# Splits of token differences set free, and the first weight sums issued behind block 1's routing

## The chip, the cores and the metric

The kernel runs on one core of a Trainium2 chip. The metric is device microseconds of one launch. Five engines work beside each other, each through a queue of its own that it takes in order: TensorE (matrix products into PSUM), VectorE and ScalarE (elementwise work, the only ones of the four that read PSUM), POOL (elementwise work in SBUF), and SyncE, which issues most DMAs.

## The reference

Three layers are computed, one after the other.

```python
# 1: attention, 4 batches, 8 heads, 576 positions, 64 wide; banded or dilated mask
x = softmax(mask(q @ k.T / 8)) @ v            # -> 2304 tokens x 512
# 2: gated layer, 512 -> 1536 -> 512
x = (sigmoid(x @ w_gate) * (x @ w_val)) @ w_out
# 3: soft routing to 8 experts with 4 slots each
logits = x @ phi                              # 2304 x 32
d = softmax(logits, over tokens); c = softmax(logits, over slots)
slot_in = d.T @ x
slot_out = relu(slot_in[e] @ w1[e]) @ w2[e]   # for each expert e
out = c @ slot_out
```

The products of layer 2 are made from two-part numbers: every operand is split into a high half (rounded to the matrix engine's single-pass float32 form, `F32R`) and a low half (the difference), and a product is the sum of high by high, high by low and low by high.

## The kernel before, in words

Tokens come in five blocks n: blocks 0 to 3 are the first 512 tokens of the four batches, block 4 gathers the last 64 of each. The 1536 features of layer 2 come in twelve groups f of 128. Attention is made for pairs of units (block, pair of heads); block 0's is first, and the others run beside the gated layer of blocks 0 and 1 (`l1`, L515).

Blocks 2 and 3 are then done as a pair (`pair_l1`, L661). Their attention results stay unsplit, `xf[2]` and `xf[3]`, and the four products of a 2 by 2 block product (weights: gate and value, each in two halves of the 512 inputs; tokens: two blocks, each in the same two halves) are made from seven products of sums, so that a feature group takes 42 matrix instructions. The token sides of these seven are b11, b21 (`pair_x2`, the halves of block 2), b22 (`pair_x3`, a half of block 3) and the differences t1 to t4. `pair_sums` (L564) makes the differences on POOL, `pair_t` (L586) splits each into halves, in two column pieces: ScalarE casts the high half, VectorE subtracts for the low one (`split`, L552). The weight sides of a group are a11, a12, a22 and sums s1 to s4: class `PairW` (L599), with `sums1` to `sums3` on VectorE, the high halves on ScalarE, the low ones on VectorE and POOL (`low1`, `low2`).

After block n's gated layer comes its routing, `Post(n)`: eighteen steps. Logits and their exponentials; shares (the softmax over slots); twelve turns, each transposing one quarter of the features' results of 128 tokens on TensorE, with a copy out of PSUM, for block 1 always on ScalarE (L826); weights; and three gathers with the accumulation into `acc` (L864). `Post(0)` runs inside block 1's loop. `Post(1)` runs between block 1 and the pair, and the list `prep` is dealt out between its steps by `Spread`: of `len(prep)` items so many after each step that all are out three steps before the end.

Order. A planner fixes each engine's queue when the program is built: of the instructions that it takes to be ready, the earliest in the program goes first, so that work traced late can run early in a gap. `keep_in_program_order` ties an instruction behind the one traced just before it on the same engine, and behind that one alone. `kp` (L549) does so while `fixed[0]` is set, and `pinned` sets it around a call. Tiles are handed out by tag, and a tile's first writer waits until the last readers of the buffer's former tile are done: the two `qk` buffers held the last attention scores, the two `v` buffers the last values, and the two `xa` buffers hold `xf[2]` and `xf[3]`, after which b22 takes the first and the sums' tile `s` the second.

Of the kernel before, what the change touches and what calls it, by code (L numbers as in the profile page):

```python
# [60 lines left out]
def tile_kernel(  # L61
# [25 lines left out]
    def b8(tag, shape, dt, name):  # L87
        return big.tile(shape, dt, tag=tag, name=name, bufs=BUFS[tag])
# [463 lines left out]
    def split(eng, hi, lo, src_):  # L552
        kp(nc.scalar.copy(hi, src_))
        kp(eng.tensor_tensor(lo, src_, hi.bitcast(F32), ALU.subtract))
# [31 lines left out]
    def pair_t(z, c):  # L586
        name, at = (("t1", (0, 0)), ("t2", (2, 0)), ("t3", (0, 1)), ("t4", (2, 1)))[z]
        if c == 0:
            t = b8(("qk", "v")[z % 2], [P, 2, 2, 512], F32R, "t_hl")
            pair[name] = t[:, 0], t[:, 1]  # L590
        hi, lo = pair[name]
        split(nc.vector, hi[:, c], lo[:, c], pair["t", at[0]][:, at[1], c])
# [427 lines left out]
        prev_w[0].high2()  # L1020
        prev_w[0].low2()

    early_prep = [(pair_sums, z) for z in range(4)] + [(pair_t, z, c) for z in range(4) for c in range(2)]
    prep = [(pair_x2, z) for z in range(4)]
    prep += [(first_w,), (pair_x3, 0), (pair_x3, 1), (first_sums,), (first_splits,)]

    def pinned(fn, *args):
        fixed[0] = True
        fn(*args)
        fixed[0] = False  # L1030

    for x in early_prep:
        pinned(*x)
    prep = [(pinned, *x) for x in prep]
    after = after[mix0.done :] + Post(1).all()
    mix = Spread(prep, [(len(after) - 3, len(prep))])
    for fn, *args in after:
        fn(*args)
        mix()
    prev = None  # L1040
    w4 = []

# [57 lines left out]
    for f in range(NF):  # L1100
        c = f % 4
# [255 lines left out]
```

## Time and profile before

| | before |
|---|---|
| median of 3 runs | 498.23 us (497.89 to 499.33) |
| profiled execution | 498.77 us, span 496.8 us, mean granted clock 0.982 |
| TensorE products busy | 470.1 us, 95% of the span |
| VectorE, ScalarE, POOL busy | 301.4, 248.6, 158.3 us |
| chain that ended last | TensorE 76%, VectorE 3%, ScalarE 3% |
| moved by DMA | 112.13 MB, mean 226 GB/s |

The span is the time from the first to the last instruction of one profiled execution; its own time is 2 us longer, and runs differ by some tenths of a per cent. A busy TensorE isn't one at full speed: its products are pipelined, and the granted clock (1.00 is 2.4 GHz, 0.50 is 1.2 GHz) stands beside it in the windows. The place that the change touches is a small part of the span, so it is read from the windows and the timelines of that place, not from the shares of the whole.

### The profile page before, as it was taken

Reading aid. Unit: us, or ns where it says so; the run is one execution under the profiler, and the core shown is the slowest. Engines: PE = TensorE matmul, PEld = TensorE weight load, DVE = VectorE, ACT = ScalarE, POOL = GpSimd, SP = SyncE. Lnnn points to the kernel's source line nnn. Section 1 sums busy time; section 2 is a strip of 40 time slices with the busy share of each in tenths; the row PEclk is TensorE's granted clock in tenths of the full one; section 3 lists DMA queues with packets and bytes.
Section 4 is the critical chain, followed back from the end, with each engine's and each line's share of the span. In section 5 each row is a group of like instructions: output and inputs, shape, how many; then the busy total and the mean of one; then the engine's idle time right before and its main releaser. Section 6 shows DMA issues by size and latency. Waiting matters only on the chain.

```text
span 496.8 us, 12732 instructions
## 1 busy us (share of the span) xinstructions
PE 470.1 (95%) x5476; PEld 357.7 (72%) x5476; DVE 301.4 (61%) x561; ACT 248.6 (50%) x428; POOL 158.3 (32%) x132
## 2 busy tenths in 40 slices
PE   6789999999899999999889999999999999999993
PEld 3468877878677877877458888888887889643552
DVE  3969698967767353555956566556557665521522
ACT  2466566747666453546855545545435544300232
POOL 0243555635383321182143243342312134010100
PEclk9989999999999999999989999999999999989998
DMA  8979898979986501750020220220699795679997
GB/s 327 405 258 335 290 369 305 322 270 364 408 289 211 172 3 49 253 195 3 0 84 2 84 86 1 86 84 0 239 383 424 288 341 191 251 257 367 421 392 219
DMA packets 23784, 112.13 MB, mean 226 GB/s; under 512 B 2352, under 2 KB 7216, under 8 KB 14640
## 3 DMA queue, kind: packets, MB, share of 16 engines
q1 hardware_dynamic: 23408, 111.06, 60.1%
q8 instruction: 43, 0.70, 0.6%
q10 hardware_dynamic: 320, 0.26, 0.2%
q14 instruction: 13, 0.11, 0.1%
HBM read 97.16 MB, written 14.16 MB: 224 GB/s over the span
## 4 chain that ended last, share of the span: by engine, by line
PE 76%; DVE 3%; ACT 3%; issue 2%; DMA 1%; POOL 1%; SPq 0%; ACTq 0%; DVEq 0%; POOLq 0%
PE l1ps L527 27%; PE pa L651 13%; PE pe L651 6%; PE tp L821 4%; PE h_ps L1123 3%; PE pd L651 3%; PE xp L208 3%; PE so_ps L1182 2%; PE sp L852 2%; PE lt_ps L785 2%; PE s_ps L145 2%; PE wt_ps L468 1%; PE tr L188 1%; PE op L1221 1%; PE si_ps L1102 1%
## 5 line engine op out<-in xcount | busy, mean ns | idle before, releaser
L527 PE MATMUL l1ps<-x_hi,whl 128*128 128x512 f32 x384 | 129.5, 404 | 3.1 <-ACT x_hi L229 2.3
L527 PEld LDWEIGHTS l1ps<-x_hi,whl 128*128 128x128 f32 x384 | 72.2, 189 | 20.4 <-ACT x_hi L229 3.0
L527 PE MATMUL l1ps<-x_lo,whl 128*128 128x512 f32 x192 | 76.1, 397 | 0.0
L442 POOL TENSOR_TENSOR fw<-fw 128x512 int32<-128x512 int32 x36 | 51.4, 1437 | 71.5 <-DVE fw L441 35.1
L527 PEld LDWEIGHTS l1ps<-x_lo,whl 128*128 128x128 f32 x192 | 36.4, 190 | 7.2 <-issue 0.4
L539 DVE TENSOR_TENSOR g<-l1ps,g 128x512 f32<-128x512 f32 (+1 forms) x36 | 21.6, 600 | 32.7 <-PE l1ps L527 32.2
L527 PE MATMUL l1ps<-x,whl 128*128 128x256 f32 x288 | 37.2, 286 | 0.0
L527 PEld LDWEIGHTS l1ps<-x,whl 128*128 128x128 f32 x288 | 35.4, 191 | 2.1 <-issue 1.9
L537 ACT ACTIVATE g<-l1ps 128x512 f32<-128x512 f32 (+1 forms) x36 | 18.9, 526 | 30.2 <-PE l1ps L527 30.1
L494 POOL TENSOR_TENSOR whl<-w,whl 128x512 fp32r<-128x512 f32 x12 | 15.9, 1326 | 52.1 <-ACT whl L493 40.6
L821 PE MATMUL tp<-cst,g 128*128 128x128 f32 x216 | 28.6, 275 | 0.0
L494 POOL TENSOR_TENSOR whl<-wst,whl 128x512 fp32r<-128x512 f32 x12 | 16.1, 1340 | 38.6 <-ACT whl L493 33.9
L439 ACT ACTIVATE fw<-st 128x512 f32<-128x512 f32 x36 | 22.7, 675 | 10.9 <-DMA st<-wd 10.9
L821 PEld LDWEIGHTS tp<-cst,g 128*128 128x128 f32 x216 | 24.1, 140 | 3.6 <-ACT g L537 1.7
L494 DVE TENSOR_TENSOR whl<-fw,whl 128x512 fp32r<-128x512 f32 x24 | 22.0, 922 | 5.8 <-ACT whl L493 5.3
L720 DVE TENSOR_TENSOR tm<-pe,tm 128x512 f32<-128x512 f32 x12 | 8.3, 692 | 27.7 <-PE pe L651 27.7
L826 ACT COPY gt<-tp 128x512 f32<-128x512 f32 x33 | 18.5, 587 | 10.9 <-PE tp L821 9.3
L441 DVE TENSOR_SCALAR fw<-st 128x512 int32<-128x512 uint32 x36 | 22.6, 654 | 1.9 <-DMA st<-wd 1.9
L208 PEld LDWEIGHTS xp<-pt_ring,v 64*64 64x64 f32 x1216 | 19.2, 135 | 6.1 <-issue 4.0
L493 ACT CAST whl<-fw 128x512 fp32r<-128x512 f32 x24 | 14.7, 619 | 17.3 <-POOL fw L442 13.2
L440 DVE TENSOR_SCALAR fw<-fw 128x512 uint32<-128x512 uint32 x36 | 20.7, 584 | 2.7 <-ACT fw L439 2.2
L208 PE MATMUL xp<-pt_ring,v 64*64 64x32 f32 (+1 forms) x1216 | 20.7, 219 | 1.6 <-issue 0.9
(464 smaller groups left out, 961.2 us busy)
## 6 DMA issues: line engine op xcount, KB each, us to landing
ew<-w SPq DMA_DIRECT2D x32, 1024.0 KB, 7.9
st<-wd SPq DMA_DIRECT2D x18, 1024.0 KB, 9.0
wst<-wg SPq DMA_DIRECT2D x12, 1024.0 KB, 6.9
v<-qkv SPq DMA_DIRECT2D x20, 512.0 KB, 6.7
wg<-fw SPq DMA_DIRECT2D x12, 512.0 KB, 7.7
w<-wg SPq DMA_DIRECT2D x6, 1024.0 KB, 7.4
qk<-qkv SPq DMA_DIRECT2D x10, 576.0 KB, 6.4
qk<-qkv SPq DMA_DIRECT2D x8, 528.0 KB, 5.5
```

The lines of the kernel that those rows point to most:

```text
L208: nc.tensor.matmul(o, lhsT=v[k, t, i, r, :], rhs=p_[k, 2 * r + t, i, 0:nq], start=True, stop=True)
L439: nc.scalar.activation(top, st[:, c, 1].bitcast(F32), AF.Prelu, scale=2.0**-112, alpha=2.0**32)
L440: nc.vector.tensor_scalar(top.bitcast(U32), top.bitcast(U32), 3, None, ALU.logical_shift_left)
L441: nc.vector.tensor_scalar(low.bitcast(I32), st[:, c, 0], 2.0**-29, None, ALU.mult)
L442: nc.gpsimd.tensor_tensor(low.bitcast(I32), top.bitcast(I32), low.bitcast(I32), ALU.add)
L494: (nc.gpsimd if pool[h] else nc.vector).tensor_tensor(whl[:, 1, h], src[:, h], whl[:, 0, h].bitcast(F32), ALU.subtract)
L527: nc.tensor.matmul(pt[:, 0:nt], lhsT=whl[:, w_, a, dc, :], rhs=x_[n][:, dc, :], start=first, stop=(dc == HP_ORDER[-1] and w_ == 1),)
L537: nc.scalar.activation(g, pt[:, 0:nt], AF.Sigmoid)
L539: nc.vector.tensor_tensor(g, pt[:, 0:nt], g, ALU.mult)
L651: nc.tensor.matmul(pt, lhsT=w[:, w_, P * c : P * c + P], rhs=x_[:, c], start=first and c == 0 and w_ == 0 and x_ is hi, stop=c == 1 and w_ ...
L821: nc.tensor.transpose(tp[:, c], g_sb[self.n, 4 * q + c][:, P * j : P * j + P], ident)
L826: nc.scalar.copy(to, tp)
```

## The change

The four difference steps of `pair_sums` stay pinned. The eight calls of `pair_t` (sixteen instructions: eight on ScalarE, eight on VectorE) are traced at the same place in the program, but no longer pinned. `first_sums` and `first_splits`, which make the sums of group 0's weights and their halves, leave the list that is dealt out between the steps of `Post(1)` and are called, pinned, after the last of its steps. The list so has seven items instead of nine.

```diff
-    early_prep = [(pair_sums, z) for z in range(4)] + [(pair_t, z, c) for z in range(4) for c in range(2)]
     prep = [(pair_x2, z) for z in range(4)]
-    prep += [(first_w,), (pair_x3, 0), (pair_x3, 1), (first_sums,), (first_splits,)]
+    prep += [(first_w,), (pair_x3, 0), (pair_x3, 1)]
 
     def pinned(fn, *args):
         fixed[0] = True
         fn(*args)
         fixed[0] = False
 
-    for x in early_prep:
-        pinned(*x)
+    for z in range(4):
+        pinned(pair_sums, z)
+    for z in range(4):
+        for c in range(2):
+            pair_t(z, c)
     prep = [(pinned, *x) for x in prep]
     after = after[mix0.done :] + Post(1).all()
     mix = Spread(prep, [(len(after) - 3, len(prep))])
     for fn, *args in after:
         fn(*args)
         mix()
+    pinned(first_sums)
+    pinned(first_splits)
     prev = None
     w4 = []
```

## Rows read from the trace of the kernel before

**Rows 1.** Windows by stage: busy us of each engine, granted clock, DMA share, GB/s.

```profile
204.00:229.00 25.00, 25.00 (x376) 20.30 (x375) 12.27 (x23) 12.08 (x21) 15.02 (x12) 1.00 0.54 198
229.00:258.00 29.00, 24.85 (x222) 15.72 (x221) 22.17 (x48) 23.59 (x46) 6.74 (x7) 0.94 0.05 15
258.00:350.00 92.00, 92.00 (x407) 76.17 (x407) 57.83 (x99) 47.60 (x88) 32.18 (x30) 1.00 0.14 53
350.00:480.00 130.00, 128.77 (x1253) 91.08 (x1251) 65.56 (x133) 45.45 (x86) 22.52 (x19) 0.99 0.84 328
```

The columns are the window, its length, then PE, PEld, DVE, ACT and POOL (TensorE's products, its weight loads, VectorE, ScalarE, POOL).

**Rows 2.** Windows of 2 us in the passage to the pair stage.

```profile
238.00:240.00 2.00, 1.09 (x11) 0.85 (x9) 1.07 (x7) 1.97 (x5) 0.00 (x0) 1.00 0.00 0
...
248.00:250.00 2.00, 0.04 (x1) 0.04 (x1) 2.00 (x5) 0.81 (x4) 0.02 (x1) 1.00 0.00 0
250.00:252.00 2.00, 2.00 (x5) 1.42 (x6) 2.00 (x6) 0.53 (x2) 0.73 (x1) 0.51 0.00 0
252.00:254.00 2.00, 2.00 (x7) 0.93 (x5) 0.95 (x3) 1.64 (x3) 1.38 (x1) 0.63 0.00 0
```

**Rows 3.** Chain of waits from 225 to 275 us: start us, us, what.

```profile
231.66 2.78 PE lt_ps L785 x96
...
238.17 1.28 ACT L805
...
243.24 2.23 DVE b_lo L554 x3
...
252.62 2.02 POOL w__3366 L613
```

**Rows 4.** Timeline of POOL: start us, us, line, operation, count, idle before.

```profile
216.66 5.03 POOL L577 TENSOR_TENSOR tsum<-xf 128x512 f32<-128x512 f32 x4
221.66 5.02 POOL L577 TENSOR_TENSOR tsum<-xf,tsum 128x512 f32<-128x512 f32 x4
...
243.31 1.01 POOL L897 COPY pm<-c 128x512 f32<-128x512 f32 x1 [16.62 <-DVE c L891]
```

**Rows 5.** Timeline of TensorE from 223 to 259 us.

```profile
223.04 0.60 PE L188 MATMUL tr<-cst,qk 128*128 128x128 f32 x4
...
227.80 0.98 PE L208 MATMUL xp<-pt_ring,v 64*64 64x16 f32 x56
228.71 1.09 PE L821 MATMUL tp<-cst,g 128*128 128x128 f32 x8
...
231.61 2.83 PE L785 MATMUL lt_ps<-g,wp 128*32 128x128 f32 x96
...
244.82 1.07 PE L852 MATMUL sp<-gt,dt 128*32 128x512 f32 x8
...
258.06 0.39 PE L651 MATMUL pa<-b_hi,w__3466 128*128 128x512 f32 x1
```

**Rows 6.** Timeline of ScalarE from 228 to 253 us.

```profile
229.37 4.26 ACT L553 CAST t_hl<-tsum 128x512 fp32r<-128x512 f32 x8
...
239.57 0.29 ACT L809 ACTIVATE d<-d 128x128 f32<-128x128 f32 x1
...
241.00 3.10 ACT L826 COPY gt<-tp 128x512 f32<-128x512 f32 x6
245.55 1.14 ACT L553 CAST b<-xf 128x512 fp32r<-128x512 f32 x2 [1.45 <-DVE b_lo L554]
...
251.72 0.83 ACT L641 CAST w__3366<-s 128x768 fp32r<-128x768 f32 x1 [1.48 <-DVE s L613]
```

**Rows 7.** Timeline of VectorE from 232 to 250 us.

```profile
232.33 4.89 DVE L554 TENSOR_TENSOR t_hl<-tsum,t_hl 128x512 fp32r<-128x512 f32 x8
237.15 0.28 DVE L793 COPY lt<-lt_ps 128x128 f32<-128x128 f32 x1
...
245.39 1.39 DVE L864 SCALAR_TENSOR_TENSOR acc<-acc,nm,sp 128x512 f32<-128x512 f32 x2
...
249.05 0.75 DVE L613 TENSOR_TENSOR s<-wst 128x256 f32<-128x256 f32 x2
```

**Rows 8.** Line L554, the low halves of b22: ns min/median/max, first and last start.

```profile
L554 DVE TENSOR_TENSOR b<-xf,b x2: 679/952/1224, 246.7 to 247.3; 128x512 fp32r<-128x512 f32 x2
```

## The prediction

> **What bounds the kernel now.** I read the windows by stage first [rows 1]. From 258 to 350 us, the twelve features of the pair stage, TensorE is busy 92.00 of 92.00 us at full clock, and DMA moves little. From 350 on DMA works at a share of 0.84, with loads that start when the pair stage gives its buffers back, so whatever moves 258 moves the end by as much. From 204 to 229 TensorE is also full, while ScalarE is busy 12.08 of 25 us and VectorE 12.27. Only 229 to 258, the passage from block 1 into the pair stage, has room: TensorE 24.85 of 29, and there ScalarE (23.59) and VectorE (22.17) are the loaded ones. The fine windows show the holes [rows 2]: 0.91 us at 238 to 240, then TensorE nearly silent from 248 to 250, and after that its granted clock at 0.51 for two microseconds (half the slices at 1.2 GHz) and 0.63 in the next two.
>
> The chain of waits says who makes them [rows 3]. It goes from the logits product over the exponentials' table load to the three low halves of x2 (243.24), then to POOL's low half of the first weight sums (252.62). The gaps are filled from the engines' own queues [rows 4 to 7]. ScalarE casts the eight high halves of the differences from 229.37 for 4.26 us, ahead of all else [rows 6]. VectorE makes their eight low halves at 232.33 for 4.89 us, and only behind them, at 237.15, copies the logits that TensorE had finished at 234.44 [rows 5, 7]. The high halves of b22 wait 1.45 us for the last x2 low half, because b22 takes the buffer of xf[2] [rows 6]. The weight sums start at 249.05 [rows 7], because their tile takes the buffer of xf[3], which the low halves of b22 read last. From 249.05 it takes until 258.06 for the first product of feature 1 [rows 5].
>
> **The change, part by part.** *Splits free to move.* The halves need POOL's differences, done from 217.9 to 226.7 us (four in 5.03 and four in 5.02 us) [rows 4], and a buffer. t1 and t3 take the two qk buffers, read last by transposes of which the second group ends at 223.6 [rows 5]; t4 takes the v buffer that the last attention sums read until 228.78 [rows 5]; t2 waits for POOL alone, until 222.9 and 224.2. Unpinned, the planner may put them into the idle queue time of 217 to 229; that it lets work traced late run early is seen in POOL's copy at 243.31, which the code issues in the last stage [rows 4]. So six of eight high halves (0.53 us each) and six of eight low halves (0.61) go in front of 229, into ScalarE's 12.9 and VectorE's 12.7 idle microseconds of that stage [rows 1]. I cost them there at nothing; what it costs if that cover fails is the last rival.
>
> VectorE below costs 0.61 us per half, but a two-input operation beside POOL stretches: the low halves of b22 ran 679 and 1224 ns, the slow one beside POOL [rows 8]. The Trainium skill, "GPSIMD Engine Reference", section 1 (Specifications), says that POOL shares its SBUF interfaces with VectorE and that VectorE operations with two SBUF inputs contend with it; the trace agrees. It speaks against the change, since the low halves now run beside POOL's differences: by that rule and the row's 0.54 us six of them cost 3.3 us more, still inside the idle 12.7, and the sum stays.
>
> *What that gives VectorE.* With two low halves left (1.2 us, before 232.4), the logits' copy runs when the product ends, 234.5 instead of 237.15: 2.65 us earlier for the maximum, the exponentials and the shares.
>
> *What it gives ScalarE.* This is where the gain is lost again. From 229.4 it has two high halves (to 230.5), then two turned copies and one x2 high half that may go behind the first of them (to 232.4). After that it has nothing: TensorE is in the logits product until 234.4 and hands over the next turned group some 0.4 later, at 234.85 (two groups take 1.09 [rows 5]). From there ScalarE has ten turned copies (six take 3.10 us [rows 6]), three x2 high halves, one weight cast and two b22 high halves, 16 at 0.525 = 8.4 us, the table load of 1.28 [rows 3] and three small exponentials of 0.2, some 0.5: 10.2 us, to 245.0. Before, the last turned copy ended at 244.10 and the b22 high halves at 246.69 [rows 6]. So 3.2 us removed end as 1.7.
>
> *The x2 and b22 halves* now come at wider steps (7 pieces over 15 steps instead of 9), so the first weight cast stands behind the sixth turned group. It is in the 10.2 us; TensorE's first products wait for it but have until the weight sums. The last x2 low half waits for the shares, 2.65 us earlier, and ends before ScalarE reaches b22 at some 242, so that wait of 1.45 goes. Three turned copies stand behind the second b22 cast, which so ends at 243.4, and its low half near 244.2.
>
> *The first sums behind all steps of block 1.* sums1 is now tied to the last accumulate of block 1's routing. Before it was not: that ended at 246.78 [rows 7], 2.3 us ahead of the sums. Now it is what comes last: turned copy 245.0, four products 1.07 [rows 5], accumulate 0.70 (two in 1.39 [rows 7]): sums at 246.9 instead of 249.05, so **2.15 us** gained. Were the tie absent, they could start at 244.2; it costs 2.7 of what the first part offers. Behind the tied sums wait ScalarE's two casts and POOL's three low halves, whom TensorE waits for; in POOL's queue they pass nothing but the copy of 243.31, since the differences stay tied where they are.
>
> *Next feature's pieces.* The first low half and the first sums of feature 1 are tied behind VectorE's previous instruction, which was the accumulate and is now sums3 of feature 0. Before, feature 1's sums ran between those of feature 0: 249.05 to the cast at 251.72 is 2.67 us [rows 6, 7]. Four sums in a row at 0.42, with a hand-over, are 1.85 by estimate: **0.8 us** gained. The bounds are 0 (all of it latency) and 1.1 (four at 0.38, the pitch of the pair in rows 7). I take 0.8, near the upper end, because two foreign sums stood in between. No DMA is issued by a moved step, and SP's queue stays as it is.
>
> The sum is 2.15 + 0.8 = 3.0 us (rounded). The profiled execution took 498.77 us (span 496.8); 3.0 less is 495.8. It lies 0.54 above the median of the runs, 498.23, so I forecast **495.2 us**, with feature 1 starting at 255.1.
>
> A second rule concerns the table load. Here the load takes 1.28 us from 238.17, and the exponential at 239.57 is the second one behind it [rows 3, 6], so nothing more stands between. The Trainium skill, "ScalarE: Activation LUTs", "What ACT_TABLE_LOAD costs", adds a drain of about 1.38 us, 2.66 in all; by it ScalarE's list would end at 246.4 and the gain would be 1.6. This trace shows no such drain.
>
> **Rivals.**
> *More of it (gain 5.4).* ScalarE's idle 232.4 to 234.85 is filled, because the planner puts turned groups in front of the logits product. Then the list ends 2.4 us earlier: 492.8. For it: two groups already run ahead of that product, eight transposes at 228.71 [rows 5]. Against it: logits have the earlier place in the program, and TensorE is full from there to the product's end. The ceiling is TensorE's idle 4.15 us [rows 1] plus what 4 us at a mean clock of 0.57 would give back, 1.7: 5.9.
> *No difference.* The freed splits stay where they were (the change does not do what it says, if the planner takes POOL or the buffers to be late), or TensorE, waiting for turned copies while ScalarE loads its table, falls to 1.2 GHz near 240 and hands the last groups over 2 us later. The sums then start around 249 and only part of the 0.8 remains: 497.5. For it: silence of 2 us brought 0.51 before. Against: 0.91 us at 238 to 240 did not [rows 2].
> *Slower: ScalarE stuck in front of POOL.* Its queue runs in order. The high halves of t2 are held by no buffer; if the planner takes POOL's differences for shorter than 1.26 us each, it places them ahead of block 1's last sigmoid and copies. ScalarE then stands until 222.9 and 224.2, the banks stay full and TensorE, busy without a hole there [rows 1], waits. Decided by whether t2's cast sits before some 219.6 in the queue: from there on at most 224.2 - 219.6 = 4.6 us are lost, with 1.0 of clock loss (half of rows 2's 2 us); against the 3.0 gained, +2.6: 500.8. Against it: t1, t3 and t4 are held by buffers past POOL's results anyway.
>
> **How the numbers follow.** Forecast 0.45 (493.7 to 496.7 by itself: the 0.8 at either end, and 1 us of misplaced ScalarE order), more 0.15, no difference 0.25, slower 0.15. A measurement of this kernel tells about 0.3%, 1.5 us, from no change. The first two lie below 496.7: faster 0.60; same 0.25; slower 0.15. The range goes from 491.8, 1 us under the larger gain and near the ceiling, to 499.2, through the no-difference case, leaving most of the slower one out.
>
> **What would show it.** Right: high halves of t1 to t3 at 219 to 229 in ScalarE's queue; logits copied near 234.5; a ScalarE hole around 232.4 to 234.8; sums near 246.9 directly behind the last accumulate; POOL's low half ending near 251.6; feature 1 at 255.1 and every later feature moved alike. Wrong: high halves still in a row behind 229; the sums starting well before the last accumulate could end, or after 249; a TensorE hole before 229; windows after 258 that no longer show a full TensorE.

## The result and the profile after

The changed kernel takes 503.29 us (median of 7 runs, 500.90 to 505.01), the kernel before 497.89 in the same comparison: a ratio of 1.009, with a 95% interval of 1.0062 to 1.0118. It is slower by 5.4 us; 495.2 had been forecast. The profiled execution took 504.05 us, with a span of 502.1 (before 496.8).

Windows by stage, after (columns as in [rows 1]):

```profile
204.00:229.00 25.00, 21.68 (x266) 17.17 (x265) 14.57 (x26) 13.97 (x25) 15.85 (x12) 0.98 0.55 200
229.00:258.00 29.00, 25.18 (x314) 16.40 (x312) 20.72 (x45) 19.74 (x39) 5.29 (x4) 0.96 0.00 1
```

Read the first line: TensorE was busy for 25.00 of 25 us there before and now for 21.68. The loss begins ahead of the passage for which the gain was forecast. Fine windows of 2 us, after, show where, and what the clock did behind it:

```profile
224.00:226.00 2.00, 0.45 (x4) 0.42 (x4) 1.87 (x2) 1.61 (x4) 2.00 (x3) 1.00 0.00 0
226.00:228.00 2.00, 0.37 (x3) 0.17 (x2) 2.00 (x4) 2.00 (x6) 1.71 (x2) 1.00 0.00 0
228.00:230.00 2.00, 2.00 (x8) 1.71 (x8) 2.00 (x4) 1.61 (x3) 0.00 (x0) 0.50 0.00 0
230.00:232.00 2.00, 2.00 (x7) 1.58 (x6) 0.78 (x2) 0.00 (x0) 0.00 (x0) 0.64 0.00 0
...
258.00:260.00 2.00, 1.89 (x6) 1.52 (x7) 0.34 (x1) 0.29 (x1) 1.62 (x3) 0.68 0.23 29
260.00:262.00 2.00, 2.00 (x6) 1.55 (x5) 0.00 (x0) 1.02 (x2) 0.90 (x1) 0.50 0.74 250
```

The timelines of the four engines, after (ScalarE, TensorE, VectorE, POOL; the bracket is the idle time ahead of an instruction and what ended it):

```profile
209.08 1.28 ACT L381 ACT_TABLE_LOAD   x1
...
215.41 0.59 ACT L826 COPY gt<-tp 128x512 f32<-128x512 f32 x1
223.16 0.62 ACT L553 CAST t_hl<-tsum 128x512 fp32r<-128x512 f32 x1 [7.16 <-POOL tsum L577]
224.39 0.62 ACT L553 CAST t_hl<-tsum 128x512 fp32r<-128x512 f32 x1 [0.61 <-POOL tsum L577]
224.91 0.58 ACT L189 COPY pt_ring<-tr 128x512 f32<-128x512 f32 x1
...
241.21 0.58 ACT L826 COPY gt<-tp 128x512 f32<-128x512 f32 x1 [2.12 <-PE tp L821]
...
253.36 1.28 ACT L703 ACT_TABLE_LOAD   x1
...
255.19 0.81 ACT L641 CAST w__3379<-s 128x768 fp32r<-128x768 f32 x1
...
225.55 0.66 PE L821 MATMUL tp<-cst,g 128*128 128x128 f32 x4 [1.68 <-ACT pt_ring L189]
227.84 0.99 PE L821 MATMUL tp<-cst,g 128*128 128x128 f32 x4 [1.63 <-DVE gt L824]
...
228.48 0.78 PE L527 MATMUL l1ps<-x_hi,whl 128*128 128x512 f32 x1
...
232.77 1.59 PE L208 MATMUL xp<-pt_ring,v 64*64 64x32 f32 x96
...
237.17 0.66 PE L821 MATMUL tp<-cst,g 128*128 128x128 f32 x4
237.75 2.83 PE L785 MATMUL lt_ps<-g,wp 128*32 128x128 f32 x96
...
258.11 1.56 PE L651 MATMUL pa<-t_hl,w__3379 128*128 128x512 f32 x4 [1.32 <-POOL w__3379 L613]
...
263.46 0.39 PE L651 MATMUL pa<-b_hi,w__3466 128*128 128x512 f32 x1
...
240.65 0.29 DVE L793 COPY lt<-lt_ps 128x128 f32<-128x128 f32 x1 [2.55 <-PE lt_ps L785]
...
249.81 1.29 DVE L554 TENSOR_TENSOR b<-xf,b 128x512 fp32r<-128x512 f32 x2
251.02 0.74 DVE L864 SCALAR_TENSOR_TENSOR acc<-acc,nm,sp 128x512 f32<-128x512 f32 x1
251.67 0.42 DVE L613 TENSOR_TENSOR s<-wst 128x256 f32<-128x256 f32 x1
...
253.02 0.69 DVE L702 TENSOR_TENSOR tm<-pd,tm 128x512 f32<-128x512 f32 x1 [0.47 <-PE pd L651]
...
216.85 5.02 POOL L577 TENSOR_TENSOR tsum<-xf 128x512 f32<-128x512 f32 x4
221.84 5.87 POOL L577 TENSOR_TENSOR tsum<-xf,tsum 128x512 f32<-128x512 f32 x4
```

What matters is the cast at 223.16 in ScalarE's part. ScalarE's queue runs in order, and at its head from 216.0 on, behind the copy of 215.41, stands t2's first cast, which reads POOL's fifth difference; that is finished at 223.1. The cast has waited 7.16 us, the second 0.61 more. Behind them stand the copy of the turned scores at 224.91 and the copies that free the PSUM banks which TensorE writes to. TensorE, which has work until 223.9, then waits 1.68 us for that copy and 1.63 us for VectorE's copy out of the next bank. VectorE is held for 6.68 us by the low half of the same tile; what that half costs by itself was not run. TensorE's work for the next four microseconds runs at a granted clock of 0.50 and 0.64 (0.50 is 1.2 GHz), after it had been busy for 0.82 of the 4 us ahead. The chain of waits names the same step; before, no POOL instruction stood in this part of it (the columns are start, us and what):

```profile
216.89 7.48 POOL tsum L577 x6
224.39 0.63 ACT t_hl L553
```

The new order of ScalarE's queue, against the old one (minus: before; plus: after):

```
 L826 COPY gt<-tp 128x512
-L189 COPY pt_ring<-tr 128x512
-L826 COPY gt<-tp 128x512
-L537 ACTIVATE g<-l1ps 128x512
...
+L553 CAST t_hl<-tsum 128x512 x2
+L189 COPY pt_ring<-tr 128x512
+L553 CAST t_hl<-tsum 128x512
+L826 COPY gt<-tp 128x512
```

**Where the 5.2 us are.** For comparing executions I count from one early instruction, the load of the exponential's table for line 381 (208.89 us before, 209.08 after; both kernels are alike up to there). Timeline of before, ScalarE, then TensorE (the first of the layer products ahead of the attention sums, and these sums):

```profile
208.89 1.28 ACT L381 ACT_TABLE_LOAD   x1
...
224.26 0.48 PE L527 MATMUL l1ps<-x_hi,whl 128*128 128x512 f32 x1
...
227.19 1.59 PE L208 MATMUL xp<-pt_ring,v 64*64 64x32 f32 x96
```

The first product of feature 1 comes 49.17 us behind it before [rows 5] and 54.38 after: 5.21 later, and the span is 5.3 longer. Of this:

- The logits product starts 28.67 behind instead of 22.72, 5.95 later. The attention sums ahead of it start 5.39 later (23.69; before 18.30). That is the two waits of 3.31, 1.36 for the layer products ahead of them at the low clock (4.29 us from 228.48 to 232.77; 2.93 for the same ones before), and 0.7 around the two groups of four transposes. The other 0.56 are four transposes that now run ahead of the logits (0.58 from 237.17).
- From the logits' end to the first weight sums it takes 11.09 us (240.58 to 251.67) instead of 14.61 (234.44 to 249.05): 3.52 regained.
- From the sums to feature 1 it takes 11.79 instead of 9.01: 2.78 lost again.

### The profile page after: what moved, and what is told of

Same layout as the page of the kernel before. It is cut to its first block, busy times and chain, and to the rows that moved or that the text cites. A ratio compares the mean times of both kernels' runs of the same rounds, so it can differ in the third digit from the quotient of the medians.

```text
span 502.1 us, 12731 instructions
## 1 busy us (share of the span) xinstructions
PE 470.7 (94%) x5476; PEld 358.2 (71%) x5476; DVE 302.2 (60%) x561; ACT 247.8 (49%) x428; POOL 160.2 (32%) x132
## 4 chain that ended last, share of the span: by engine, by line
PE 75%; ACT 4%; POOL 3%; DVE 3%; issue 2%; DMA 1%; DVEq 0%; ACTq 0%; SPq 0%
PE l1ps L527 25%; PE pa L651 13%; PE pe L651 6%; PE tp L821 4%; PE so_ps L1186 3%; PE h_ps L1127 3%; PE sp L852 3%; PE pd L651 3%; PE xp L208 2%; PE lt_ps L785 2%; PE s_ps L145 2%; POOL tsum L577 1%; PE wt_ps L468 1%; PE op L1225 1%; PE tr L188 1%
## 5 line engine op out<-in xcount | busy, mean ns | idle before, releaser
L821 PE MATMUL tp<-cst,g 128*128 128x128 f32 x216 | 29.7, 278 | 3.3 <-ACT pt_ring L189 1.7
L145 PE MATMUL s_ps<-qk 64*32 64x64 f32 x1280 | 16.3, 225 | 5.5 <-issue 3.5
```

The costliest lines, as they stand in the source:

```text
L145: return nc.tensor.matmul(to, lhsT=u["qk"][d, 128 * t + 32 * i : 128 * t + 32 * i + 32], rhs=u["qk"][d, 512 + o : 512 + o + 64], start=Fal ...
L821: nc.tensor.transpose(tp[:, c], g_sb[self.n, 4 * q + c][:, P * j : P * j + P], ident)
```

## The experiments

Times of the kernel before in the three comparisons: 498.42 us (23 runs; for e1 to e4), 498.28 (33; e5 to e8) and 498.05 (29; e9 to e11). The last three columns are offsets from the table load named above, each of one execution.

| run | median us | ratio, interval | attention sums | logits | feature 1 |
|---|---|---|---|---|---|
| before | | | 18.30 | 22.72 | 49.17 |
| after | 503.29 | 1.009, 1.0062 to 1.0118 | 23.69 | 28.67 | 54.38 |
| e1_splits_only | 502.40 | 1.0067, 1.0043 to 1.0092 | 23.70 | 28.69 | 53.55 |
| e2_sums_only | 497.43 | 0.9974, 0.9951 to 0.9998 | 18.31 | 22.73 | 48.58 |
| e3_t2_behind_turn | 497.35 | 0.9977, 0.9953 to 1.0001 | 18.32 | 24.16 | 48.25 |
| e4_t2_alone_free | 504.02 | 1.0103, 1.0070 to 1.0136 | 23.40 | 27.82 | 53.17 |
| e5_pool_order | 498.68 | 1.0012, 0.9985 to 1.0038 | 19.64 | 24.89 | 50.62 |
| e6_tied_and_sigmoid | 495.87 | 0.9944, 0.9918 to 0.9970 | 18.42 | 24.20 | 47.58 |
| e7_tied_low_sigmoid | 495.09 | 0.9932, 0.9903 to 0.9960 | 18.44 | 23.42 | 46.81 |
| e8_sums_and_sigmoid | 496.82 | 0.9975, 0.9951 to 0.9999 | 18.30 | 22.72 | 48.23 |
| e9_tied_splits_only | 497.52 | 0.9988, 0.9967 to 1.0008 | 18.37 | 23.36 | 48.23 |
| e10_s2_low_on_vector | 498.70 | 1.0011, 0.9987 to 1.0035 | 18.34 | 23.32 | 49.75 |
| e11_s2_low_and_add | 494.63 | 0.9942, 0.9917 to 0.9967 | 18.33 | 23.32 | 45.29 |

In these executions the granted clock falls for some microseconds in after, e1, e4, e5, e10 and before, and stays at 1.00 through the passage in the others. In before the fall, at 250 to 254 [rows 2], costs nothing at feature 1: the next four products, at 254.69, wait for POOL's low half all the same [rows 3]. The offsets of e2, e3, e6 to e9 and e11 can so be set beside each other and beside before's.

**The two parts by themselves.** e1 takes the splits' part alone, e2 the sums' part alone.

```diff
 e1, against after
-    prep += [(first_w,), (pair_x3, 0), (pair_x3, 1)]
+    prep += [(first_w,), (pair_x3, 0), (pair_x3, 1), (first_sums,), (first_splits,)]
...
-    pinned(first_sums)
-    pinned(first_splits)
 e2, against after
-            pair_t(z, c)
+            pinned(pair_t, z, c)
```

> The splits are free, but the first sums and their halves are dealt out between the steps of block 1's routing as before. Theory (ScalarE stands in its queue behind the cast of t2, which waits for POOL's third difference, and block 1's sigmoid, turned copies and then TensorE wait behind it): the stall is all here, ScalarE idle some 7 us in front of the first split, TensorE idle some 3.5 us at 223 to 228 and at half clock after it, 502 to 504 us. Rival (the loss is made by the sums tied behind the last accumulate, with the sigmoid's table load and TensorE's slow clock behind them): the stall is hidden, no later than 498 us.

> The splits are pinned as before, the first sums and their halves stand behind all steps of block 1's routing. Theory (stall behind t2's cast): TensorE full from 204 to 229 as before, 497 to 499 us, the sums moved by no more than 1 us either way. Rival (the tied sums make the loss): 501 to 504 us, the time lost between the last turned copy and feature 1.

The loss is in e1, with the same late attention sums as after; e2 is slightly faster than before, by an interval that hardly excludes no change. In e2 nothing ahead of the logits moves.

**One cast pair freed, and the same pair tied.** e4 is the kernel before with t2's two splits alone free; e3 is the changed kernel with t2's two casts ordered behind the copy of the last turned scores (an order within ScalarE's queue, no added wait).

```diff
 e4, against before
     for x in early_prep:
-        pinned(*x)
+        if x[0] is pair_t and x[1] == 1:
+            x[0](*x[1:])
+        else:
+            pinned(*x)
 e3, against after
-        nc.scalar.copy(pt_ring[:, u["z"] % 4].rearrange("p c i q -> p c (i q)"), tr)
+        turned = nc.scalar.copy(pt_ring[:, u["z"] % 4].rearrange("p c i q -> p c (i q)"), tr)
+        if pool is ps_a:
+            last_turn[0] = turned
...
+            tc.add_manual_dep(high.ins, behind.ins.name, ...)
...
-        split(nc.vector, hi[:, c], lo[:, c], pair["t", at[0]][:, at[1], c])
+        split(nc.vector, hi[:, c], lo[:, c], pair["t", at[0]][:, at[1], c], last_turn[0] if z == 1 else None)
```

> As the kernel before, but the two calls that split t2 are not pinned; the other six, and the first sums, are as before. Theory (stall behind t2's cast): these two casts alone go in front of block 1's last sigmoid and wait for POOL; TensorE idle 3 to 5 us at 223 to 228, 501 to 503.5 us. Rival (low halves beside POOL): two low halves at most beside POOL, less than 1 us, 497 to 499 us.

> As the changed kernel, but the two casts of t2 are tied in ScalarE's queue behind the copy of the last turned attention scores (at 223.7 us before); all other halves stay free. Theory (stall behind t2's cast): ScalarE has six casts in front of block 1's last copies without a wait over 1 us, TensorE full from 204 to 229, the 5.4 us come back: 497 to 498.5 us if the passage behind is as in the changed kernel (0.7 us shorter than before), 495.2 us if the prediction's sum for the passage holds. Rival (VectorE's low halves and POOL's differences hinder each other): they still run beside each other, so 501 us or more.

ScalarE and TensorE in e4, timeline; t2's two splits bring the whole loss without any other freed split:

```profile
224.58 0.62 ACT L553 CAST t_hl<-tsum 128x512 fp32r<-128x512 f32 x1 [7.17 <-POOL tsum L577]
...
226.97 0.66 PE L821 MATMUL tp<-cst,g 128*128 128x128 f32 x4 [1.69 <-ACT pt_ring L189]
```

With the casts tied (e3) the attention sums are back at 18.32 and the time is 497.35, 5.9 below the changed kernel's (which was timed in another comparison). So the cause is shown from both sides. What is left is a gain of 0.9 at feature 1, not 3.0, and by its time e3 can't be told from the kernel before. Timeline of e3, TensorE, VectorE, POOL:

```profile
227.51 1.59 PE L212 MATMUL xp<-pt_ring,v 64*64 64x32 f32 x96
...
230.91 1.92 PE L863 MATMUL sp<-gt,dt 128*32 128x512 f32 x16 [0.79 <-DVE x L408]
...
221.04 3.19 DVE L565 TENSOR_TENSOR t_hl<-tsum,t_hl 128x512 fp32r<-128x512 f32 x2
...
225.18 0.75 DVE L565 TENSOR_TENSOR t_hl<-tsum,t_hl 128x512 fp32r<-128x512 f32 x1
226.19 3.73 DVE L565 TENSOR_TENSOR t_hl<-tsum,t_hl 128x512 fp32r<-128x512 f32 x3 [0.25 <-ACT t_hl L557]
...
221.94 6.83 POOL L588 TENSOR_TENSOR tsum<-xf,tsum 128x512 f32<-128x512 f32 x4
```

Here is a second cost. Of these six low halves on VectorE five run beside POOL's differences, which end at 228.77: four of the five take 1.45 to 1.78 us each from start to end and one takes 0.75, where eight took 4.89 us in all by themselves [rows 7]. POOL's four take 6.83 instead of 5.02 [rows 4]. VectorE so comes late to the low halves of the attention (L408), and TensorE waits 0.79 us for them.

**A dose of the same cause.** In e5 POOL makes the differences in the order 0, 2, 1, 3, so that t2's come third and fourth instead of fifth and sixth, two operations (2.5 us) sooner.

```diff
-    for z in range(4):
+    for z in (0, 2, 1, 3):
         pinned(pair_sums, z)
```

> As the changed kernel, but POOL makes the differences in the order t1's, t2's, t3's, t4's, so that t2's two pieces are done 2.5 us sooner (near 220.6 and 221.8 instead of 223.1 and 224.4). The queues of the other engines are the same. Theory (ScalarE stands behind t2's cast until POOL is done): ScalarE and VectorE go on 2.5 us sooner, TensorE idles at most 1 us at 223 to 228 instead of 3.4, its clock does not fall there, and 3 to 5 us come back: 498.5 to 500.5 us. Rival (low halves and differences hinder each other): no change, 502 to 504 us.

The wait of ScalarE in e5:

```profile
220.34 0.62 ACT L553 CAST t_hl<-tsum 128x512 fp32r<-128x512 f32 x1 [4.62 <-POOL tsum L577]
```

The wait is 2.54 us shorter, the attention sums come 4.05 sooner than after and the time falls to that of before. 1.5 us more comes back than the wait, 1.36 of it since TensorE keeps its full clock: the layer products ahead of the attention sums take 2.93 us (225.49 to 228.42), as before. At feature 1 e5 is still 1.45 us behind before; there its own clock fell, to 0.58 and 0.57 from 254 to 258.

**The rest of the missing gain.** e6 adds to e3 that feature 0's first sigmoid keeps its place in ScalarE's queue; after has it, with its table load, between the casts of the first sums (253.36). e7 adds to e6 that the low halves of t2 and t3 stand behind the last low halves of the attention on VectorE.

```diff
 e6, beside e3's edit
-        kp(nc.scalar.activation(g2, m1, AF.Sigmoid))
+        kept(nc.scalar.activation(g2, m1, AF.Sigmoid))
 e7, beside e6's edit
-                nc.vector.tensor_tensor(lo, xp[y], hi.bitcast(F32), ALU.subtract)
+                last_split[0] = nc.vector.tensor_tensor(lo, xp[y], hi.bitcast(F32), ALU.subtract)
...
+        tie(kp(eng.tensor_tensor(lo, src_, hi.bitcast(F32), ALU.subtract)), low_behind)
```

> As the kernel with t2 behind the turned scores (497.35 us), and feature 0's first sigmoid, with its table load, is tied behind ScalarE's previous instruction in the program, so that it no longer runs between the casts of the first sums. Theory (sums, casts and POOL's low half are the chain there; table load and sigmoid stand 1.9 us in it): 1.8 us less, 495.5 us, feature 1 at 255.6 instead of 257.4. Rival (POOL's low half or VectorE's sums set the end): no more than 0.5 us less, 497 us.

> As the kernel before it in this list, and the four low halves of t2 and t3 are tied in VectorE's queue behind block 1's last attention halves, so that they no longer run beside POOL's differences. Theory (beside POOL the low halves stretch and hold up VectorE's part of the last attention halves, for which TensorE waits 0.8 us and the logits product comes 1.4 us late): the logits product starts at 232.0 instead of 233.35, 494.2 us. Rival (VectorE's four low halves only move behind, where they delay the logits copy by as much): no change against the kernel before it.

> Splits pinned as before, sums behind block 1's routing (497.43 us), and feature 0's first sigmoid tied as in the two kernels before. Theory (the sigmoid's table load stands in the chain of the first sums, 1.8 us): 495.6 to 496 us. Rival (the sums wait for the b22 low halves, so the sigmoid is hidden): 497 us or more.

The timeline of ScalarE in e6 (the last cast of the first sums, now ahead of the table load), and of TensorE in e7:

```profile
250.35 0.83 ACT L652 CAST w__3379<-s 128x768 fp32r<-128x768 f32 x1 [1.46 <-DVE s L624]
...
251.99 1.28 ACT L714 ACT_TABLE_LOAD   x1
```

```profile
229.18 1.92 PE L866 MATMUL sp<-gt,dt 128*32 128x512 f32 x16
```

The sigmoid behind the casts gives 0.67 at feature 1 on top of e3, where 1.8 had been expected, and the low halves behind the attention's 0.77 more: the wait of 0.79 is gone. With both, 495.09 us is reached, about what had been forecast for the change itself, but by two edits which the forecast did not have; this does not bear out its sum. The times of e6 and e7 alone, 0.8 apart, don't tell them apart; the offsets do. In e8, e2 with the sigmoid kept, the same edit gives 0.35 at feature 1 and nothing that the times can tell.

**Is the tie of the sums dear?** e9 is e7 without the sums' part, so the first sums are dealt out among the routing's steps again (the sigmoid's edit is out too; it stands behind the casts of the sums there anyway).

```diff
-    prep += [(first_w,), (pair_x3, 0), (pair_x3, 1)]
+    prep += [(first_w,), (pair_x3, 0), (pair_x3, 1), (first_sums,), (first_splits,)]
...
-    pinned(first_sums)
-    pinned(first_splits)
```

> The splits free but tied as in the 495.09 us kernel (casts of t2 behind the last turned scores, low halves of t2 and t3 behind the last attention halves), and the first sums dealt out between the routing's steps as in the kernel before; here the planner puts the sigmoid behind the casts of the sums by itself. Theory (the sums wait for the low halves of b22 either way, so their tie to the last accumulate costs little, and feature 1's low half and sums run between feature 0's again): 495.5 to 496.5 us. The prediction's own step (the tie costs 2.7 us): 492.4 us.

VectorE in e9, timeline:

```profile
245.61 0.74 DVE L878 SCALAR_TENSOR_TENSOR acc<-acc,nm,sp 128x512 f32<-128x512 f32 x1
246.26 0.42 DVE L627 TENSOR_TENSOR s<-wst 128x256 f32<-128x256 f32 x1
246.97 0.69 DVE L627 TENSOR_TENSOR w__3466<-wst,w__3466 128x512 fp32r<-128x512 f32 x1 [0.29 <-ACT w__3466 L641]
```

Freed of the tie, the sums still start right behind the last accumulate, so the tie holds up nothing to speak of. But the pieces of feature 1 come between feature 0's sums again, and feature 1 starts 1.4 us later than in e7. Of this 0.79 lie behind the start of the sums (10.26 us to feature 1, in e7 9.47), which is the order. The other 0.63 lie ahead of it: the sums themselves start 37.97 us behind the table load, in e7 37.34. The x2 halves are dealt out in other places with nine pieces than with seven; that this is the reason wasn't shown. The 1.4 is what the sums' part is worth here, and the time, 497.52, is 1.0 above what had been expected for e9.

**Two more steps.** e10 is e7 with one of POOL's three last low halves given to VectorE; e11 is e10 with VectorE's addition of the pd products (L702 in after) kept in its place behind the sums.

```diff
 e10, beside e7's edits
-        prev_w[0].low2()
+        w0 = prev_w[0]
+        w0.sub(nc.vector, w0.w2[:, 1, 0], w0.s[:, 1], w0.w2[:, 0, 0].bitcast(F32))
+        w0.sub(nc.gpsimd, w0.w2[:, 1, 1:3], w0.s[:, 2:4], w0.w2[:, 0, 1:3].bitcast(F32))
 e11, beside e10's edits
-        kp(nc.vector.tensor_tensor(m1, pd, m1, ALU.add))
+        kept(nc.vector.tensor_tensor(m1, pd, m1, ALU.add))
```

> As the 495.09 us kernel, but of the first weight sums' low halves, which POOL makes in one instruction of 2.0 us, VectorE makes s2's (256 columns), and POOL only those of s3 and s4. Theory (TensorE's last wait in the passage is for POOL's low half): s2's low half lands some 0.5 us behind the cast instead of 2.9, 1.3 to 1.8 us less, 493.5 us. Rival (s4's low half on POOL is as late): 0.3 us less at most, 494.8 us.

> As the kernel before it in this list, and VectorE's addition of feature 0's first two products is tied behind its previous instruction, so that it no longer stands between the second and the third of the first weight sums, where it waits for TensorE. Theory (the sums are the chain): 1.1 us less again, 492.4 us. Rival (TensorE's own products set the end by then): the same time as the kernel before it.

e10 missed. Its wait for POOL's low half is gone, but another is there, ScalarE and TensorE in its timeline:

```profile
254.08 0.40 ACT L645 CAST w__3467<-s 128x256 fp32r<-128x256 f32 x1 [2.58 <-DVE s L627]
...
256.33 0.57 ACT L727 COPY tm<-pa 128x512 f32<-128x512 f32 x1
...
256.95 2.81 PE L665 MATMUL pa<-t_hl,w__3379 128*128 128x512 f32 x6 [2.86 <-ACT tm L727]
```

It is the changed kernel's fault on a small scale: a cast that waits 2.58 us for feature 1's sums stands at the head of ScalarE's queue, and the copy that frees TensorE's bank stands behind it. The clock fell behind that hole as well (0.78 and 0.50 from 256 to 260), so the 2.9 us by which feature 1 starts later than in e7 are not the wait alone. In e11 that copy comes ahead of the table load, and VectorE makes feature 0's four sums in a row (timeline, VectorE):

```profile
246.28 0.42 DVE L627 TENSOR_TENSOR s<-wst 128x256 f32<-128x256 f32 x1
...
247.54 0.42 DVE L627 TENSOR_TENSOR s<-wst 128x256 f32<-128x256 f32 x1
```

At 494.63 us it has the lowest median of all and beats both kernels, though not by as much as expected (492.4). From e7, which starts feature 1 1.5 us later, its time can't be told apart: the ratios are 0.9942 and 0.9932.

## Why the prediction was wrong, step by step

- **"Six of eight high halves ... go in front of 229 ... I cost them there at nothing."** This step failed. Six casts came by 229.35, and as cover I counted ScalarE's idle time by its amount, 12.9 us. Idle time covers an instruction only if its input is there when the queue reaches it. t2's cast was at the head at 216.0 and its input came at 223.1; the attention sums came 5.39 us later by it, and in e3, with only this cast pair tied, 0.02. The hole in TensorE ahead of 229 is the sign that the prediction named for being wrong. The step was seen and put down as the slower rival, with a chance of 0.15.
- **The rival's price, +2.6.** The place and the mechanism were right: t2's cast, held by no buffer, in the queue ahead of 219.6. The loss of at most 4.6 with 1.0 of clock was near: 5.39 at the attention sums, of which about 1.4 clock. The larger error was to set the whole 3.0 of the forecast's gain against it; e3, in which the stall is gone, has 0.9 of it. "Against it: t1, t3 and t4 are held by buffers" was no argument, since e4 shows that one freed tile suffices. The clock of 0.51 at 250 to 252 was misread on the way: 0.50 is 1.2 GHz, so nearly all of that window ran slow, not half of it. The price of 1.0 for two such microseconds holds.
- **Low halves beside POOL, "still inside the idle 12.7, and the sum stays".** The stretch was of about the priced size (3.3 for six): in e3 six took 7.67 us, 4.0 over 0.61 each, the last of them after POOL was done. That it stays hidden was wrong, by the same confusion of idle time with free time: VectorE's L408 stood behind them, and e7 gets 0.77 back. The Trainium skill, "GPSIMD Engine Reference", section 1 (Specifications), says that POOL shares its SBUF interfaces with VectorE, and that VectorE operations with two SBUF inputs contend with it. The trace agrees, and POOL pays as well: its four differences stretched from 5.02 to 6.83.
- **VectorE's logits copy as the product ends.** Right in relation: 240.65 for a product that ends at 240.58; before, 2.71 us lay between [rows 5, 7].
- **ScalarE's hole and its list of 10.2 us.** The hole came (2.12 us ahead of 241.21). The list behind it was shorter, 7.9 us to 249.1, because one copy and one x2 high half more than forecast went ahead of it, and the two b22 high halves came behind the last copy. So the sums start 11.09 behind the logits' end; forecast were 12.5.
- **The first sums, 2.15 earlier.** With the stall taken away this holds: in e3 the sums start 38.08 us behind the table load, 2.08 earlier than before (40.16), though by two errors that cancel, logits 1.44 later and 1.37 less behind them.
- **"It costs 2.7", the tie behind the last accumulate.** Wrong, at most 0.65. VectorE itself is in b22's low halves until 251.02, just ahead of that accumulate, and e9, without the tie, starts its sums right behind the same accumulate.
- **"Four sums in a row ... 0.8 us gained."** It turned into 2.78 lost. The four sums aren't in a row: VectorE's addition of pd came between (253.02), 0.43. The sigmoid with its table load came ahead of the last cast, 0.42, and the same order made two of TensorE's products late, 0.39. The low clock at 258 to 262 makes 1.6 (5.35 us from 258.11 to feature 1; e3 has 3.75 for the same products at 1.00). e11 shows that the term was there to be had: its sums take 1.71 us to the cast, forecast was 1.85.
- **The drain behind a table load.** No drain in after either: the load of line 805 at 242.33 takes 1.28 us and the next activation starts at 243.62. The Trainium skill, "ScalarE: Activation LUTs", "What ACT_TABLE_LOAD costs", would put a drain of about 1.38 us there. The trace disagrees, and none of the loss is that.

Two things stay open. Why the planner sets t2's casts where it does wasn't read out; that it counts on POOL's results far sooner than they come would explain it, but only the order was seen. And why the clock fell at 258 to 262 is not shown. It isn't the stall: e1 and e4 have the stall and kept a granted clock of 1.00 from 234 on. Nor is it the pair of waits ahead of these products alone (0.66 and 1.32 us): with 0.66 and 1.31 e3 kept 1.00 and e5 fell to 0.58.

## What to carry to other kernels

Idle microseconds of an in-order engine are no cover for an instruction whose input comes late: for each freed instruction compare when its input is ready with when the queue reaches it, and look at what stands behind it. One pair of instructions placed too early lost more here than all the others gained; an order edge behind the last urgent instruction kept the freedom and took the loss away. Where a change frees several things, undo them one at a time: here the losing piece was t2's two casts, and the change with three such order edits (e7) gave 3.2 us.

## What the runs showed of the hardware

Two things had not been expected. That VectorE slows down beside POOL had been, at 0.54 us a low half; but POOL slows down too. A low half, 0.68 us from start to end by itself, took 1.45 to 1.78 for four of five in e3, and each of POOL's four differences beside them took 1.72 to 1.75, where before all eight took 1.27 to 1.29. And the clock fell behind quite similar holes in some traces only. TensorE was busy for 2.05 of the 4 us ahead of 258 in after, and for 2.03 of the 4 us ahead of 254 in e3; the clock went to 0.68 and 0.50 in the first, and stayed at 1.00 in the second:

```profile
250.00:252.00 2.00, 1.34 (x6) 0.76 (x5) 1.97 (x7) 1.99 (x5) 0.33 (x1) 1.00 0.00 0
252.00:254.00 2.00, 0.69 (x3) 0.30 (x2) 1.92 (x1) 0.38 (x1) 2.00 (x2) 1.00 0.00 0
254.00:256.00 2.00, 2.00 (x10) 1.64 (x9) 0.00 (x0) 1.09 (x2) 1.21 (x2) 1.00 0.36 41
```

So 1.6 us between two single traces of these kernels can be the clock alone, and a step of that size is better read from medians.
